# A Winograd convolution with batch norm and SiLU on one core: unit outputs in a tile of three parts, and a new order of work around the second unit

## The chip, the cores and the metric

The kernel runs on one core of one Trainium2 chip. The metric is the device time of one execution in microseconds, taken as the median of several; lower is better. A profile of one execution shows, for each engine, when each instruction ran.

The engines are TensorE (PE; its weight loads are shown apart as PEld), VectorE (DVE), ScalarE (ACT), GpSimd (POOL) and SyncE (SP, which here only issues DMAs).

## The reference

A convolution of width 3 along the sequence, then a batch norm with fixed statistics, then SiLU. x is 2 x 2048 x 1024, w is 3 x 1024 x 1024, both bfloat16.

```python
xp = jnp.pad(x, ((0, 0), (P, P), (0, 0)))
y = sum(jnp.einsum('bsc,cd->bsd', xp[:, k:k + S, :], w[k]) for k in range(K))
inv_std = 1.0 / jnp.sqrt(var + 1e-5)
y = (y - mean) * (g * inv_std) + b
return _silu(y)
```

## The kernel before

It is a Winograd scheme: six outputs along the sequence are made from eight products. 342 blocks of six cover a sequence of 2048.

**Stage 1, transforms.** For each of the two sequences, 17 windows of x come in by DMA, and TensorE multiplies them with the constant matrix Rm (line 230) into PSUM. ScalarE and VectorE copy the result to T_sb (lines 244 and 246): eight transformed values (j = 0 to 7) for each channel tile and block. In the second sequence a window is made in three thirds, and matmuls of unit 0 are put between them (lines 401 to 408, the generator `first`, advanced by `run(first, n)`).

**The weights.** The output channels come in eight chunks of 128 (dc = 0 to 7). For j = 0 and 7 the raw weights are used (tile wch). For j = 1 to 6 they are made by GpSimd: `pair_sum` adds the outer two taps (line 163), and `pair_tap` adds or subtracts the middle one (line 173) into the tile uch. That is three sums and six taps for a chunk. `scale_weights` makes scaled taps w2x, w1x, w0x on ScalarE (line 151). For chunks 2 to 7 the first of the three sums is made on VectorE by a reduction (`outer_by_reduce`, line 169). uch has two buffers, so the chunk that is made follows the chunk that is used.

**Stage 2, units.** A unit is one chunk of one sequence: 16 units, numbered 0 to 15, with chunk and sequence in that order (unit 2 is chunk 1 of the first sequence). A unit is eight groups of eight matmuls of 342 columns (line 255), in the order j = 1, 3, 2, 4, 5, 7, 6, 0. They go to four PSUM banks, called A, B, C and G: A1, B3, A2, B4, C5, G7, C6, A0. The even units use banks 0 to 3, the odd ones 4 to 7. Unit 0 has another order (its groups of 7 and 0 come in parts of 231 and 111 columns, its last group is C6), and the last unit is cut in two.

Between the groups, `copy_out` (line 303) lets ScalarE copy a bank to a tile: m1 after A1, m3 after B3, s1 after A2, s2 after B4, m5 after C5. A2 adds to bank A, which m1 must have been copied out of, and in the same way B4 follows m3, and C6 follows m5. VectorE then makes the six outputs y[0] to y[5] of the unit by sums with a factor (line 296): d1 after s1, then y[2] and y[4] after B4, then y[1], y[3], y[5], then y[5] with G (line 342), then y[2] and y[4] again after C6, y[1], y[3], y[5] again, and y[0] last, after A0.

**The order on ScalarE.** The finished outputs go through SiLU on ScalarE (`silu`, line 266) into yT, in three calls: outputs 2 and 4, then 1, 3 and 5, then 0. A unit does not issue its own calls, since its sums are not done. It leaves them in the list `late`, and the next unit takes them from there: `pace` says how many entries are taken ahead of each of its copies m1, m3, s1, s2, m5, and what is left is taken behind m5. With the usual pace (1, 0, 1, 1, 0) the order on ScalarE is call, m1, m3, call, s1, call, s2, m5. Unit 1 has (0, 1, 1, 1, 0). Behind the three calls stands `finish`, which issues the DMA transpose of yT on the SP queue (line 425) and the stores of the unit before (lines 439 and 443). There are two yT tiles, used in turns.

**The dependencies.** Each unit opens a new tile y with one buffer (line 292). Its first write waits until the calls on the tile before are all done. In that tile output i stands in row i, so the calls read rows with a step of two.

**Chunk 1.** While unit 1 runs, the weights of chunk 1 are made (line 476 to 478): `sums(0, 2, 1)` scales taps 2 and 1 and makes the first sum and two taps, `sums(1)` the second, and `sums(2, 0)` scales tap 0 (w0x) and makes the third; the last of these is put at the end of `late`. The weights of chunk 2 are made from unit 3 on in program order (lines 459 to 467), with its reduction on VectorE ahead of unit 2 (line 458).

Of the kernel before, what the change touches and what calls it, by code (L numbers as in the profile page):

```python
# [10 lines left out]
FP32 = mybir.dt.float32  # L11
# [17 lines left out]
BETA = -4.0 / 5.0  # L29
M_OUT = 6  # L30

ENDS = (2, 4, 0, 5, 1, 3)
NJ = 8
WT = 21
# [3 lines left out]
def kernel(  # L38
# [13 lines left out]
    P = 128  # L52
    CT = C // P
    DC = D // P
    assert S % P == 0 and C % P == 0 and D % P == 0
    NTB = (S + M_OUT - 1) // M_OUT
# [27 lines left out]
    def load_weights(dp):  # L84
        open_weights(dp)
        for k in (0, 2, 1):
            nc.sync.dma_start(out=pair_tile[dp][:, k], in_=w_all[:, k, :, dp * 2 * P:(dp + 1) * 2 * P])
# [174 lines left out]
            )  # L262
            yield

    def silu(dc, yT, y_all, c0, c1, i0, i1, step=1):
        nc.scalar.activation(  # L266
            yT[:, i0:i1:step, c0:c1],
            y_all[:, i0:i1:step],
            ACT.Silu,
            bias=beta[:, dc:dc + 1],  # L270
            scale=sk[:, dc:dc + 1],
        )

    def unit(dc, bi, c0, c1, banks, yT, late, pace=(1, 0, 1, 1, 0), cut=None, calls=None):

        nn = c1 - c0
        A, B_, C_, G = [ps_all[:, k * 512:k * 512 + nn] for k in banks]
        bA, bB, bC, bG = banks
        pace = list(pace)

        def et(name):
            return epool.tile([P, NTB], FP32, name=name)[:, 0:nn]

        m1, m3, m5, s1, s2, d1 = (et(n) for n in ("m1", "m3", "m5", "s1", "s2", "d1"))
        y_all = epool.tile([P, M_OUT, NTB], FP32, name="y")[:, :, 0:nn]
        y = [y_all[:, i if calls is None else ENDS.index(i)] for i in range(M_OUT)]

        def stt(o, i0, s, i1, op1=ALU.add):
            nc.vector.scalar_tensor_tensor(out=o, in0=i0, scalar=s, in1=i1, op0=ALU.mult, op1=op1)  # L296
            load["dve"] += 0.00123 * nn

        def copy_out(dst, src):
            for _ in range(pace.pop(0)):  # L300
                if late:
                    late.pop(0)()
            nc.scalar.copy(dst, src)  # L303
            load["act"] += 0.001 * nn

        if cut:


            p0 = et("s2")
            yield from mms(bG, 7, dc, bi, c0, c0 + cut, True)  # L310
            yield from mms(bC, 0, dc, bi, c0, c0 + cut, True)
            yield from mms(bC, 0, dc, bi, c0 + cut, c1, True, cut)
            copy_out(p0, C_)
        yield from mms(bA, 1, dc, bi, c0, c1, True)
        copy_out(m1, A)
        yield from mms(bB, 3, dc, bi, c0, c1, True)
        copy_out(m3, B_)
        yield from mms(bA, 2, dc, bi, c0, c1, False)
        copy_out(s1, A)
        stt(d1, m1, 2.0, A, op1=ALU.subtract)  # L320
        yield from mms(bB, 4, dc, bi, c0, c1, False)
        if cut:
            stt(y[0], B_, ALPHA, p0)
            stt(y[2], B_, ALPHA * 4.0, s1)
            nc.vector.tensor_tensor(y[0], A, y[0], op=ALU.add)
            stt(y[4], B_, ALPHA * 16.0, s1)
        else:
            copy_out(s2, B_)
            for i in (2, 4):
                stt(y[i], B_, ALPHA * 2.0 ** i, s1)  # L330
        stt(B_, m3, 2.0, B_, op1=ALU.subtract)
        yield from mms(bC, 5, dc, bi, c0, c1, True)
        copy_out(m5, C_)
        while late:
            late.pop(0)()
        for i in (1, 3, 5):
            stt(y[i], B_, ALPHA * 2.0 ** i, d1)
        if cut:
            yield from mms(bG, 7, dc, bi, c0 + cut, c1, True, cut)
        else:  # L340
            yield from mms(bG, 7, dc, bi, c0, c1, True)
        nc.vector.tensor_tensor(y[5], G, y[5], op=ALU.add)  # L342
        yield from mms(bC, 6, dc, bi, c0, c1, False)
        for i in (2, 4):
            stt(y[i], C_, BETA * 0.5 ** i, y[i])
        stt(G, m5, 2.0, C_, op1=ALU.subtract)
        if not cut:
            yield from mms(bA, 0, dc, bi, c0, c1, False)
        for i in (1, 3, 5):
            stt(y[i], G, BETA * 0.5 ** i, y[i])  # L350
        if cut:
            stt(y[0], C_, BETA, y[0])
        else:
            stt(y[0], s2, ALPHA, A)
            stt(y[0], C_, BETA, y[0])

        if calls is None:
            late.extend(lambda i=i: silu(dc, yT, y_all, c0, c1, *i, 2) for i in ((2, 5), (1, 6), (0, 1)))
        else:
            late.extend(lambda i=i: silu(dc, yT, y_all, c0, c1, *i) for i in calls)  # L360

    def run(gen, n=None):
        while n is None or n > 0:
            if next(gen, run) is run:
                return
            if n is not None:
                n -= 1
# [3 lines left out]
    with tc.tile_pool(name="xwin", bufs=10) as xpool:  # L371
        first = unit(0, 0, 0, NTB, (0, 1, 2, 3), yTs[0], late, cut=11 * WT)
        for wi in range(NWIN):
            window = load_window(xpool, 0, wi)
            if wi in (3, 8, NWIN - 1):
                load_chunk(0, {3: 2, 8: 0, NWIN - 1: 1}[wi])
            for h in range(2):
                bk = (2 * wi + h) % 4 * 2 if wi < 10 else (0, 6, 4)[(2 * wi + h - 20) % 3]
                transform(0, wi, window, 4 * h, 4, bk, 2, 2 if h == 0 and wi in (4, 9) else 0)
            if wi == 0:  # L380
                turn_params()
            if wi == 5:
                open_chunk(0)
                scale_weights(0, (2,), on_gpsimd=True)
            if wi == 8:
                pair_sum(0, 0)
                pair_sum(0, 1)
                scale_weights(0, (0,), on_gpsimd=True)
                pair_sum(0, 2)

            run(first, {13: 2, 14: 2, 15: 4, 16: 8}.get(wi, 0))
        pair_tap(0, 0, ALU.add)
        scale_weights(0, (1,), on_gpsimd=True)
        for n, op in ((1, ALU.add), (0, ALU.subtract), (1, ALU.subtract), (2, ALU.add), (2, ALU.subtract)):
            pair_tap(0, n, op)
        make_params()
        load["act"] = load["dve"] = 0.0
        gi, done = 0, 0


        for wi in range(NWIN):
            window = load_window(xpool, 1, wi)
            for ct0, n in ((0, 3), (3, 3), (6, 2)):
                transform(1, wi, window, ct0, n, 4 + gi if gi < 4 else (4, 5, 6, 7, 2)[(gi - 4) % 5], 3)
                gi += 1
                want = 8 * gi // 3 if gi < 4 else 8 + 20 * (gi - 3) // (3 * NWIN - 3)
                run(first, want - done)
                done = want
        for k in (0, 2, 1):
            load_chunk(1, k)  # L410
        load_weights(1)
        run(first)

    opool = ctx.enter_context(tc.tile_pool(name="opool", bufs=3))
# [36 lines left out]
            store_unit(*turned.pop(0))  # L451

    late.append(lambda: finish(0, 0, yTs[0]))
    for ui, (dc, bi) in enumerate(units[1:-1], 1):
        yT = yTs[ui % 2]
        half = 4 * (ui % 2)
        if bi == 0 and dc + 1 < DC:
            outer_by_reduce(dc + 1)
        if bi == 1 and dc + 1 < DC:
            open_chunk(dc + 1)  # L460
            if dc:
                scale_weights(dc + 1)
                for n in range(3):
                    if n:
                        pair_sum(dc + 1, n)
                    for op in (ALU.add, ALU.subtract):
                        pair_tap(dc + 1, n, op)
            else:

                def sums(n, *taps):  # L470
                    scale_weights(1, taps)
                    pair_sum(1, n)
                    for op in (ALU.add, ALU.subtract):
                        pair_tap(1, n, op)

                sums(0, 2, 1)
                sums(1)
                late.append(lambda: sums(2, 0))
        calls = ((0, 2), (2, 6)) if ui == len(units) - 2 else None
        run(unit(dc, bi, 0, NTB, (half, half + 1, half + 2, half + 3), yT, late, (1, 0, 1, 1, 0) if ui > 1 else (0, 1, 1, 1, 0), calls=calls))  # L480
        if ui < len(units) - 2:
            late.append(lambda dc=dc, bi=bi, yT=yT: finish(dc, bi, yT))
        if bi == 1 and dc % 2 == 1 and (dc + 3) // 2 < DC // 2:
            load_weights((dc + 3) // 2)
# [98 lines left out]
        copy(o_before[0:n1 - n0, :, nb], pv[0:n1 - n0])  # L583
    store_unit(*units[-2], lambda nb: o_before[:, :, nb])

    y2 = epool.tile([P, M_OUT, NTB], FP32, name="y")[:, :, 0:NTB - cut]
    second = last_part(cut, NTB, there, y2, {
        "s1": [lambda: silu(dc, yT, y1, 0, cut, 0, 3)],
        "m5": [lambda: silu(dc, yT, y1, 0, cut, 3, 6)],
# [46 lines left out]
```

## Time and profile before

| | us |
|---|---|
| median of three runs | 191.4 (191.17 to 191.7) |
| the profiled execution | 191.42 |
| its span, from the first to the last instruction | 189.7 |
| first matmul of unit 2 | 49.88 |
| first matmul of unit 3 | 59.60 |

The span is what the profile covers; some 1.7 us of the time lie outside of it. In the page's rows, a time behind the bar is busy time and mean duration, and what follows the second bar is the idle time ahead of the group with what ended it. In a timeline the columns are start, time from the first start to the last end, engine, line, operation, tiles written and read, shapes and count; rows of like instructions are merged. Matmuls are pipelined, so the distance of two starts is what one costs TensorE, and not its duration.

### The profile page before, as it was taken

The page shows a single profiled execution, that of the slowest core. Times are in us where ns is not written, and L with a number is a line of the kernel's source. Part 1 is how long each engine was busy: PE and PEld are TensorE (multiplying, and loading weights), DVE is VectorE, ACT ScalarE, POOL GpSimd, SP SyncE. Part 2 cuts the span into 40 slices and gives each one's busy share as a digit, 9 for nine tenths or more (in the row PEclk, how much of TensorE's full clock was granted, in tenths as well). Part 3 has the DMA queues.
Part 4 walks back from the last instruction along what each step waited for, and adds up shares of the span by engine and source line. Part 5 has one row for each costly group of instructions (what it writes and reads, how often), then busy time and mean ns, then how long its engine had stood idle before and what let it go on. Part 6 is the DMA issues. An engine that isn't in the chain of part 4 may idle for free.

```text
span 189.7 us, 3974 instructions
## 1 busy us (share of the span) xinstructions
PE 179.5 (95%) x1424; PEld 126.5 (67%) x1424; DVE 159.2 (84%) x342; ACT 123.0 (65%) x205; POOL 148.8 (78%) x91
## 2 busy tenths in 40 slices
PE   7887999999999999999999999999999999999960
PEld 3656889766666666666666666666666666669960
DVE  6567699796999799969996999699969987879980
ACT  3787799658387827862876387648755874534680
POOL 6529999999769997999699969996999699901010
PEclk9999999999999999999999999999999999999996
DMA  5999999950609197979292889793747465656345
GB/s 131 326 351 309 334 385 262 247 132 0 124 19 202 34 209 209 208 175 208 58 200 46 191 229 205 167 204 75 164 80 157 91 147 98 137 110 154 87 114 111
DMA packets 86757, 31.72 MB, mean 167 GB/s; under 512 B 73357, under 2 KB 82578, under 8 KB 86738
## 3 DMA queue, kind: packets, MB, share of 16 engines
q1 hardware_dynamic: 86637, 31.46, 70.6%
q8 instruction: 11, 0.18, 0.4%
q14 instruction: 9, 0.07, 0.1%
q10 hardware_dynamic: 68, 0.01, 0.0%
q0 software_dynamic: 32, 0.01, 0.0%
HBM read 14.82 MB, written 8.39 MB: 122 GB/s over the span
## 4 chain that ended last, share of the span: by engine, by line
PE 74%; DVE 10%; DMA 5%; ACT 4%; issue 3%; SPq 2%; DVEq 0%; ACTq 0%
PE ps_all L255 66%; PE ps_all L230 7%; DVE y L296 6%; DMA xw<-in_x_dram 5%; SPq L215 1%; ACT T_sb L244 1%; DVE ps_all L296 1%; ACT yT L266 1%; PE ps_all L499 1%; DVE y L342 1%; DVE T_sb L246 0%; ACT s L303 0%; SPq L90 0%; ACT o_end L594 0%; DVE e L169 0%
## 5 line engine op out<-in xcount | busy, mean ns | idle before, releaser
L255 PE MATMUL ps_all<-T_sb,uch 128*128 128x342 bf16 (+2 forms) x816 | 120.8, 299 | 0.7 <-ACT m L303 0.3
L255 PEld LDWEIGHTS <-uch 128*128 128x128 bf16 x816 | 77.0, 97 | 35.3 <-issue 1.5
L266 ACT ACTIVATE yT<-y,beta,sk 128x684 bf16<-128x684 f32 (+4 forms) x46 | 44.0, 959 | 27.0 <-DVE y L296 27.0
L255 PE MATMUL ps_all<-T_sb,wch 128*128 128x342 bf16 (+4 forms) x288 | 43.7, 292 | 0.0
L296 DVE SCALAR_TENSOR_TENSOR y<-ps_all,y 128x342 f32<-128x342 f32 x90 | 41.8, 507 | 1.0
L173 POOL TENSOR_TENSOR uch<-e,wch 128x1024 bf16<-128x1024 f32 x16 | 33.9, 2134 | 9.1 <-PE ps_all L255 4.7
L173 POOL TENSOR_TENSOR uch<-e,w1x 128x1024 bf16<-128x1024 f32 x16 | 33.8, 2130 | 0.6
L173 POOL TENSOR_TENSOR uch<-eh,w1x 128x1024 bf16<-128x1024 f32 x16 | 33.8, 2132 | 0.5
L255 PEld LDWEIGHTS <-wch 128*128 128x128 bf16 x288 | 26.7, 97 | 10.9
L303 ACT COPY m<-ps_all 128x342 f32<-128x342 f32 x45 | 19.8, 442 | 19.5 <-PE ps_all L255 19.0
L244 ACT CAST T_sb<-ps_all 128x672 bf16<-128x672 f32 (+5 forms) x48 | 26.0, 619 | 5.5 <-PE ps_all L230 5.1
L230 PE MATMUL ps_all<-Rm,xw 128*128 128x168 bf16 (+1 forms) x272 | 26.4, 236 | 2.1 <-DMA xw<-in_x_dram 0.9
L246 DVE CAST T_sb<-ps_all 128x504 bf16<-128x504 f32 (+4 forms) x37 | 24.0, 694 | 5.1 <-PE ps_all L230 4.2
L230 PEld LDWEIGHTS <-xw 128*128 128x128 bf16 (+1 forms) x272 | 20.7, 99 | 7.3 <-issue 2.5
L296 DVE SCALAR_TENSOR_TENSOR y<-ps_all,d 128x342 f32<-128x342 f32 x45 | 20.3, 508 | 0.5
L163 POOL TENSOR_TENSOR eh<-w0x,wch 128x1024 f32<-128x1024 bf16 x8 | 17.0, 2128 | 1.1 <-ACT w0x L151 1.0
L296 DVE SCALAR_TENSOR_TENSOR y<-ps_all,s 128x342 f32<-128x342 f32 x31 | 14.5, 508 | 3.4 <-ACT s L303 3.2
L163 POOL TENSOR_TENSOR e<-wch,w2x 128x1024 f32<-128x1024 bf16 x8 | 17.0, 2129 | 0.0
L296 DVE SCALAR_TENSOR_TENSOR d<-m,ps_all 128x342 f32<-128x342 f32 x15 | 7.6, 508 | 10.2 <-ACT s L303 10.2
L296 DVE SCALAR_TENSOR_TENSOR ps_all<-m,ps_all 128x342 f32<-128x342 f32 x30 | 15.3, 508 | 0.0
L169 DVE TENSOR_REDUCE e<-wch 128x1024 f32<-128x2048 bf16 x6 | 13.7, 2277 | 0.0
L303 ACT COPY s<-ps_all 128x342 f32<-128x342 f32 x30 | 13.1, 435 | 0.5 <-PE ps_all L255 0.5
(69 smaller groups left out, 85.9 us busy)
## 6 DMA issues: line engine op xcount, KB each, us to landing
xw<-in_x_dram SPq DMA_DIRECT2D x30, 256.0 KB
out_dram<-o_sb SPq DMA_DIRECT2D x30, 192.0 KB
wch<-in_w_dram SPq DMA_DIRECT2D x9, 512.0 KB
out_dram<-o_sb SPq DMA_DIRECT2D x15, 120.0 KB
wch<-in_w_dram SPq DMA_DIRECT2D x6, 256.0 KB
xw<-in_x_dram SPq DMA_DIRECT2D x2, 224.0 KB
out_dram<-o_sb SPq DMA_DIRECT2D x15, 7.5 KB
out_dram<-o_sb SPq DMA_DIRECT2D x15, 0.5 KB
```

Source lines behind the costliest of these rows:

```text
L163: engine.tensor_tensor(e, a, c, op=ALU.add)
L169: nc.vector.tensor_reduce(e, taps.rearrange("p k ct d -> p ct d k"), axis=mybir.AxisListType.X, op=ALU.add)
L173: nc.gpsimd.tensor_tensor(wts[dc][:, 2 * n + (op == ALU.subtract)], outer[dc, n], odd, op=op)
L215: nc.sync.dma_start(out=xw[0:kk, :], in_=x[bi, t_lo:t_hi + 1, :])
L230: nc.tensor.matmul(banks[:, at:at + NJ * ntile], lhsT=xw[0:kk, (ct0 + c) * P:(ct0 + c + 1) * P], rhs=Rm[0:kk, :, 0:ntile], start=True, sto ...
L244: nc.scalar.copy(dst, src)
L246: nc.vector.tensor_copy(dst, src)
L255: nc.tensor.matmul(ps_all[:, bk * 512 + at:bk * 512 + at + c1 - c0], lhsT=lhsT, rhs=T_sb[bi][:, ct, j, c0:c1], start=start and ct == 0, st ...
L266: nc.scalar.activation(yT[:, i0:i1:step, c0:c1], y_all[:, i0:i1:step], ACT.Silu, bias=beta[:, dc:dc + 1], scale=sk[:, dc:dc + 1],)
L296: nc.vector.scalar_tensor_tensor(out=o, in0=i0, scalar=s, in1=i1, op0=ALU.mult, op1=op1)
L303: nc.scalar.copy(dst, src)
L342: nc.vector.tensor_tensor(y[5], G, y[5], op=ALU.add)
```

## The change

1. All units share one tile y, made once. Its rows are ordered by the calls: outputs 2 and 4 first, then 0, then 1, 3 and 5 (`KEPT`). Each SiLU call reads adjacent rows, and a write needs only the calls on its own rows to be done. The last unit's second part uses the same tile.
2. Unit 1's pace is (0, 1, 0, 1, 1), and unit 2's is (0, 1, 1, 1, 0). `sums(2, 0)` stands at the head of `late`, so it is what unit 1 takes ahead of m3: w0x comes between m1 and m3, the first SiLU call ahead of s2, the second ahead of m5, the third behind it. In unit 2, m1 comes ahead of the first call.
3. Chunk 2's first sum is a `pair_sum` on GpSimd ahead of its taps; the reduction ahead of unit 2 is gone. Chunks 3 to 7 keep theirs.
4. Two matmuls of unit 0 come one third of a window sooner, in the last window of the second sequence. Ahead of unit 0's last group (C6) stand the first three matmuls of unit 1's A1 (`begun`, in bank 4).

```diff
+KEPT = (2, 4, 0, 1, 3, 5)
 ENDS = (2, 4, 0, 5, 1, 3)
...
-    def silu(dc, yT, y_all, c0, c1, i0, i1, step=1):
+    y_all = epool.tile([P, M_OUT, NTB], FP32, name="y")
+
+    def silu(dc, yT, y_from, c0, c1, i0, i1, outputs=None):
         nc.scalar.activation(
-            yT[:, i0:i1:step, c0:c1],
-            y_all[:, i0:i1:step],
+            yT[:, outputs or slice(i0, i1), c0:c1],
+            y_from[:, i0:i1, 0:c1 - c0],
...
-        y_all = epool.tile([P, M_OUT, NTB], FP32, name="y")[:, :, 0:nn]
-        y = [y_all[:, i if calls is None else ENDS.index(i)] for i in range(M_OUT)]
+        y = [y_all[:, (KEPT if calls is None else ENDS).index(i), 0:nn] for i in range(M_OUT)]
...
-        yield from mms(bA, 1, dc, bi, c0, c1, True)
+        yield from begun or mms(bA, 1, dc, bi, c0, c1, True)
...
-            late.extend(lambda i=i: silu(dc, yT, y_all, c0, c1, *i, 2) for i in ((2, 5), (1, 6), (0, 1)))
+            parts = ((0, 2, slice(2, 5, 2)), (3, 6, slice(1, 6, 2)), (2, 3, slice(0, 1)))
+            late.extend(lambda i=i: silu(dc, yT, y_all, c0, c1, *i) for i in parts)
...
-                want = 8 * gi // 3 if gi < 4 else 8 + 20 * (gi - 3) // (3 * NWIN - 3)
+                want = 8 * gi // 3 if gi < 4 else 8 + 20 * (gi - 3) // (3 * NWIN - 3) + 2 * (gi > 3 * NWIN - 3)
...
         load_weights(1)
+
+        run(first, 7 * CT - done)
+        begun = mms(4, 1, *units[1], 0, NTB, True)
+        run(begun, 3)
         run(first)
...
+    paces = {1: (0, 1, 0, 1, 1), 2: (0, 1, 1, 1, 0)}
...
-        if bi == 0 and dc + 1 < DC:
+        if bi == 0 and 2 < dc + 1 < DC:
             outer_by_reduce(dc + 1)
...
-                    if n:
+                    if n or dc == 1:
                         pair_sum(dc + 1, n)
...
-                late.append(lambda: sums(2, 0))
+                late.insert(0, lambda: sums(2, 0))
...
-        run(unit(dc, bi, 0, NTB, (half, half + 1, half + 2, half + 3), yT, late, (1, 0, 1, 1, 0) if ui > 1 else (0, 1, 1, 1, 0), calls=calls))
+        run(unit(dc, bi, 0, NTB, (half, half + 1, half + 2, half + 3), yT, late, paces.get(ui, (1, 0, 1, 1, 0)), None, calls, begun if ui == 1 else None))
...
-    y2 = epool.tile([P, M_OUT, NTB], FP32, name="y")[:, :, 0:NTB - cut]
+    y2 = y_all[:, :, 0:NTB - cut]
```

More of the change, by code (lines that the diff above doesn't have):

```diff
@@ L272, in silu, with unit @@
         )
-    def unit(dc, bi, c0, c1, banks, yT, late, pace=(1, 0, 1, 1, 0), cut=None, calls=None):
+    def unit(dc, bi, c0, c1, banks, yT, late, pace=(1, 0, 1, 1, 0), cut=None, calls=None, begun=None):
         nn = c1 - c0
```

## The prediction

> **What bounds the kernel now.** I read the page first, then the chain of waits in order of time, then TensorE's timeline around the places where that chain leaves TensorE.
>
> ```profile
> PE 179.5 (95%) x1424; PEld 126.5 (67%) x1424; DVE 159.2 (84%) x342; ACT 123.0 (65%) x205; POOL 148.8 (78%) x91
> PE 74%; DVE 10%; DMA 5%; ACT 4%; issue 3%; SPq 2%; DVEq 0%; ACTq 0%
> ```
>
> ```profile
> 62.15 115.58 PE ps_all L255 x816
> ```
>
> TensorE is busy for 95% of the span. The second fence is the chain in order of time: from 62.15 us it is TensorE alone for 115.58 us, so whatever makes that stretch begin sooner ends the kernel sooner, and nothing inside it can be gained by a change to other engines. What is left to gain lies ahead of 62.15. TensorE's timeline (start, time until the last one ends, count) shows it:
>
> ```profile
> 35.06 0.32 PE L255 MATMUL ps_all<-T_sb,uch 128*128 128x342 bf16 x1
> 35.31 0.30 PE L230 MATMUL ps_all<-Rm,xw 33*128 33x48 bf16 x5
> ...
> 38.61 0.55 PE L255 MATMUL ps_all<-T_sb,wch 128*128 128x111 bf16 x8
> 39.30 7.25 PE L255 MATMUL ps_all<-T_sb,uch 128*128 128x342 bf16 x48
> 46.40 1.32 PE L255 MATMUL ps_all<-T_sb,wch 128*128 128x342 bf16 x8
> ...
> 49.88 2.49 PE L255 MATMUL ps_all<-T_sb,uch 128*128 128x342 bf16 x16
> 52.64 3.64 PE L255 MATMUL ps_all<-T_sb,uch 128*128 128x342 bf16 x24 [0.28 <-ACT m L303]
> 56.12 1.32 PE L255 MATMUL ps_all<-T_sb,wch 128*128 128x342 bf16 x8
> ...
> 59.60 6.20 PE L255 MATMUL ps_all<-T_sb,uch 128*128 128x342 bf16 x40
> 65.64 1.32 PE L255 MATMUL ps_all<-T_sb,wch 128*128 128x342 bf16 x8
> ...
> 69.11 5.97 PE L255 MATMUL ps_all<-T_sb,uch 128*128 128x342 bf16 x40
> 74.93 1.32 PE L255 MATMUL ps_all<-T_sb,wch 128*128 128x342 bf16 x8
> ```
>
> ```profile
> L255 PE MATMUL ps_all<-T_sb,wch 128*128 128x111 bf16 x16 | 1.4, 213 | 0.0
> ```
>
> Matmuls overlap, so I go by starts. From 52.64 to 56.12 there are 24 of them: 3.48/24 = 0.145 us each, 1.16 us a group of eight, 9.28 a unit. With that step each row says when the next one should start: 35.06 + 0.145 = 35.21, it is 35.31 (0.10 lost); the eight narrow ones step by (0.55 − 0.21)/7 = 0.049, so 38.61 + 0.39 = 39.00, it is 39.30 (0.30 lost); 39.30 + 48 × 0.145 = 46.26, it is 46.40 (0.14); 49.88 + 16 × 0.145 = 52.20, it is 52.64 (0.44); 59.60 + 40 × 0.145 = 65.40, it is 65.64 (0.24). From 69.11, 74.91 is due and 74.93 comes: nothing. The five holes hold 1.22 us, all that this change can reach.
>
> Four of them have their cause on ScalarE, whose copy out of a bank must end before TensorE adds to that bank:
>
> ```profile
> 38.81 0.44 ACT L303 COPY m<-ps_all 128x342 f32<-128x342 f32 x1 [1.88 <-PE ps_all L255]
> ...
> 41.82 0.44 ACT L303 COPY m<-ps_all 128x342 f32<-128x342 f32 x1 [0.67 <-PE ps_all L255]
> 42.73 0.96 ACT L266 ACTIVATE yT<-y,beta,sk 128x684 bf16<-128x684 f32 x1 [0.47 <-DVE y L296]
> 43.60 0.42 ACT L303 COPY m<-ps_all 128x342 f32<-128x342 f32 x1
> 44.55 1.24 ACT L266 ACTIVATE yT<-y,beta,sk 128x1026 bf16<-128x1026 f32 x1 [0.53 <-DVE y L296]
> 45.70 0.42 ACT L303 COPY s<-ps_all 128x342 f32<-128x342 f32 x1
> 46.02 0.67 ACT L266 ACTIVATE yT<-y,beta,sk 128x342 bf16<-128x342 f32 x1
> ...
> 47.25 1.07 ACT L151 ACTIVATE w0x<-wch 128x1024 bf16<-128x1024 bf16 x1
> 51.30 0.96 ACT L266 ACTIVATE yT<-y,beta,sk 128x684 bf16<-128x684 f32 x1 [2.98 <-DVE y L296]
> 52.17 0.77 ACT L303 COPY m<-ps_all 128x342 f32<-128x342 f32 x2
> ...
> 60.81 0.96 ACT L266 ACTIVATE yT<-y,beta,sk 128x684 bf16<-128x684 f32 x1 [1.14 <-DVE y L296]
> 61.68 0.95 ACT L303 COPY m<-ps_all 128x342 f32<-128x342 f32 x2
> ```
>
> The copy at 38.81 (m5 of unit 0) ends at 39.25, just ahead of 39.30. The other three copies (m3 at 43.60, m1 at 52.17 and at 61.68) stand behind a SiLU call that waits for VectorE's last sums of the unit before. So VectorE is late, ScalarE waits in its queue for it, and TensorE for ScalarE.
>
> **The change part by part.** I place the changed program's queues on these rows. A copy starts 0.20 us behind its group (38.61 to 38.81), I allow up to 0.26.
>
> *Two matmuls sooner, three of unit 1 ahead of the last group.* No matmul is added. Two of unit 0's stand after the last window's first third, where 0.10 was lost: −0.10. Three of unit 1's first group stand behind the narrow ones: they start at 38.90, the last group of unit 0 follows at 38.90 + 0.435 = 39.335, and m5 ends at 39.15, so it isn't held. Before, it began at 39.30 with these three still to do: −0.40 for both holes. The three write bank 4, whose last transform is among those at 35.31, 3.6 us earlier.
>
> *Copies ahead of SiLU in unit 1, w0x sooner.* The last group of unit 0 ends at 40.495, the other five of A1 at 41.22; TensorE's groups then start at 41.22 (B3), 42.38 (A2), 43.54 (B4), 44.70 (C5), 45.86 (G7), 47.02 (C6), and unit 2 at 49.34. ScalarE: m1 at 41.45; w0x at its end, 41.9, by its 1.07 until 42.9; m3 42.9 to 43.3, 0.2 ahead of B4: the 0.14 are gone. s1 at 43.8, the two-part SiLU 0.32 later (45.70 to 46.02) at 44.1, s2 0.87 later (42.73 to 43.60) at 45.0, the three-part SiLU at 45.3, m5 1.15 later (44.55 to 45.70) at 46.45, done at 46.9. C6 needs it at 47.02. That is the tightest place of the change, 0.1 us; taken at nothing. If the calls took their whole durations (0.96, 0.43, 1.24) m5 would end at 47.2 and 0.2 be given back; ends −0.14 and +0.1 for this part, and I take −0.14, since the starts of like pairs are nearest.
>
> *Outputs in one tile of three parts.* It removes waits: the first sums of a unit need only the call on their own part, no longer the unit's last call.
>
> ```profile
> 43.16 1.78 DVE L296 SCALAR_TENSOR_TENSOR y<-ps_all,y 128x342 f32<-128x342 f32 x4
> ...
> 47.06 0.94 DVE L296 SCALAR_TENSOR_TENSOR y<-ps_all,s 128x342 f32<-128x342 f32 x2 [0.39 <-ACT s L303]
> ...
> 53.96 2.28 DVE L169 TENSOR_REDUCE e<-wch 128x1024 f32<-128x2048 bf16 x1
> ...
> 59.85 0.92 DVE L296 SCALAR_TENSOR_TENSOR y<-ps_all,y 128x342 f32<-128x342 f32 x2
> ```
>
> In unit 1 the sums of 47.06 can start when s1, B4 and the two-part call are done, 45.1; from there VectorE runs 1.9 us ahead of before, and stops only for TensorE. In unit 2, m1 comes ahead of any SiLU: A1 ends at 50.50, m1 at about 51.2, A2 is due at 51.66: −0.44.
>
> *Chunk 2's first sum on GpSimd.* Without the 2.28 us at 53.96, unit 2's sums on C6 start when that group ends, 49.34 + 7 × 1.16 = 57.46, near 57.7 instead of 59.85 (1.2 behind their group), and end at 58.6. ScalarE gets through m5 (55.4) and three scalings at 1.07 by 59.0. The SiLU ahead of unit 3's m1 then ends by 59.95, A1 ends at 59.78, so m1 runs 60.0 to 60.4 and A2 is due at 60.94: −0.24.
>
> ```profile
> 34.61 2.12 POOL L163 TENSOR_TENSOR e<-wch 128x1024 f32<-128x1024 bf16 x1
> ...
> 48.40 2.13 POOL L163 TENSOR_TENSOR eh<-w0x,wch 128x1024 f32<-128x1024 bf16 x1 [0.98 <-ACT w0x L151]
> ...
> 56.38 4.24 POOL L173 TENSOR_TENSOR uch<-e,wch 128x1024 bf16<-128x1024 f32 x2 [1.53 <-PE ps_all L255]
> ...
> 69.16 4.23 POOL L173 TENSOR_TENSOR uch<-eh,w1x 128x1024 bf16<-128x1024 f32 x2
> ```
>
> GpSimd pays 2.12 more (its like at 34.61), but w0x at 42.9 spares it the 0.98 ahead of 48.40, and 1.53 were idle ahead of 56.38 (the sum on VectorE ended at 56.24). So its taps of chunk 2 start at 56.38 − 0.98 − 1.53 + 2.12 + 0.1 (one more start) = 56.1, 0.3 sooner. The last it must meet is unit 4's C5, due at 69.11 + 4.64 − 1.22 = 72.53, whose tap (the first half of 69.16, done at 71.3) is now done at 71.0: 1.5 to spare. Were w0x no help, it would be 72.0, still in time. Cost nothing; beyond 1.5 late it would cost TensorE its whole lateness.
>
> A rule speaks against this step. The Trainium skill (SBUF — State Buffer, "SBUF: two separate sides") has GpSimd and VectorE lock a shared port pair for a whole instruction when VectorE reads two SBUF inputs. By it nothing happens to sums with one input in PSUM; were they locked all the same, the rival "GpSimd holds VectorE" below has the result.
>
> *The store of unit 0.*
>
> ```profile
> 46.76 11.30 SPq L425 DMA_TRANSPOSE o_sb<-yT  x2
> ```
>
> Its transpose starts when the one-part call ends, at 47.5 instead of 46.76; the call that writes that yT again comes at 58.6. SP has nothing else queued but the next transpose: no cost.
>
> Sum: 0.40 + 0.14 + 0.44 + 0.24 = 1.22. The profiled execution took 191.42 (span 189.7 and 1.7 around it); the median is 191.40. Forecast 191.42 − 1.22 = **190.2**.
>
> **The rivals.**
> *ScalarE's queue of unit 1 is the new wait.* For it: 0.1 us to spare at m5, and two SiLU calls, 2.2 us, now between s1 and m5. Against: both find their sums ready (44.94 was VectorE's last). If m5 is 0.3 to 0.5 late, 0.2 to 0.4 come back: 190.4 to 190.6.
> *GpSimd holds VectorE.* If its sum at 53.9 to 56.0 blocks VectorE, unit 2's sums are as late as under the reduction, and the 0.24 stay: 190.45. Against: the two sums at 59.85 took 0.92 us inside GpSimd's row from 56.38 to 60.62, the two at 47.06 took 0.94 while GpSimd was partly idle.
> *The start is sooner, the end isn't.* TensorE runs 1.22 ahead, GpSimd only 0.3; if a later chunk is late, or stores, most is given back: 190.9 to 191.4. Against: GpSimd needs 8 × 2.13 = 17.0 us for a chunk, TensorE 18.56, and it idles between chunks.
> *Slower: the SiLU calls on parts take longer.* They recur in all units; the place is m1 behind the two-part call:
>
> ```profile
> 69.45 0.96 ACT L266 ACTIVATE yT<-y,beta,sk 128x684 bf16<-128x684 f32 x1 [3.12 <-DVE y L296]
> ...
> 70.53 0.45 ACT L303 COPY m<-ps_all 128x342 f32<-128x342 f32 x1
> ```
>
> ```profile
> L266 ACT ACTIVATE yT<-y_end,beta,sk 128x687 bf16<-128x687 f32 x2 | 1.9, 966 | 0.0
> ```
>
> m1 ends at 70.98, A2 is due at 69.11 + 2.32 = 71.43: 0.45 to spare, the point from which it decides. Twice the 0.96 would cost 0.5 in some 11 units, 5.5 in all: 195.7. Against: a call that reads adjacent rows takes 966 ns for 687 elements, the strided one 0.96 us for 684.
>
> **How the numbers follow.** Forecast 68%, ScalarE's queue 15%, GpSimd holding VectorE 4%, end not sooner 9%, slower 4%. About 0.3% (0.57 us) can be told from no change here, so faster ends at 190.83. The first three lie below it; I take 7 points off for the spread of the runs (191.17 to 191.7) and larger sizes: faster 0.80, same 0.15, slower 0.05. The range: the forecast with that spread starts at 189.8; up to 190.9 any 0.7 us of the holes may stay open.
>
> **What would show it.** Right: no hole on TensorE between 35 and 66 us; unit 2's first matmul at 49.3 and unit 4's at 67.9; w0x near 41.9; GpSimd's new sum ahead of 56; VectorE without a reduction near 54. Wrong: a start of C6 in unit 1 behind 47.1 with m5 as releaser, a wait for uch in unit 4, or an end that did not move with 67.9.

## The result, and the profile after

The changed kernel takes 190.06 us (median of six runs, 189.64 to 190.36) beside 191.45 for the kernel before (six runs, 191.17 to 192.32): a ratio of 0.9919 with a 95% interval from 0.9896 to 0.9943. The forecast was 190.2. The profiled execution took 190.36, 1.06 less than the 191.42 of the one before; its span is 188.6 us.

The page's first row and its chain, and the one piece of the chain in order of time that answers to the 115.58 us of before. The changed file's lines are some further down: L257 is the line of the matmuls (L255 before), L309 the copies, L272 SiLU, L302 the sums.

```profile
PE 179.3 (95%) x1424; PEld 126.7 (67%) x1424; DVE 157.1 (83%) x341; ACT 122.8 (65%) x205; POOL 150.9 (80%) x92
PE 87%; DMA 5%; ACT 2%; SPq 2%; DVE 1%; issue 0%; ACTq 0%; DVEq 0%
```

```profile
35.92 140.74 PE ps_all L257 x995
```

The stretch in which nothing but TensorE sets the end now begins at 35.92 instead of 62.15. VectorE had 10% of the chain and has 1%. Its busy time is 2.1 us less and GpSimd's 2.1 more: the sum that moved. TensorE's timeline:

```profile
34.65 0.49 PE L232 MATMUL ps_all<-Rm,xw 128*128 128x168 bf16 x5
35.08 0.61 PE L257 MATMUL ps_all<-T_sb,uch 128*128 128x342 bf16 x3
35.62 0.30 PE L232 MATMUL ps_all<-Rm,xw 33*128 33x48 bf16 x5
...
38.62 0.56 PE L257 MATMUL ps_all<-T_sb,wch 128*128 128x111 bf16 x8
39.02 7.14 PE L257 MATMUL ps_all<-T_sb,uch 128*128 128x342 bf16 x48
45.99 1.32 PE L257 MATMUL ps_all<-T_sb,wch 128*128 128x342 bf16 x8
...
49.47 5.97 PE L257 MATMUL ps_all<-T_sb,uch 128*128 128x342 bf16 x40
58.76 5.97 PE L257 MATMUL ps_all<-T_sb,uch 128*128 128x342 bf16 x40
...
68.05 5.97 PE L257 MATMUL ps_all<-T_sb,uch 128*128 128x342 bf16 x40
```

Read with the same step of 0.145: 38.62 + 0.39 = 39.01, it is 39.02; 39.02 + 48 × 0.145 = 45.98, it is 45.99; unit 2 takes 58.76 − 49.47 = 9.29 and unit 3 takes 68.05 − 58.76 = 9.29, a unit without a hole (9.28). Four holes are gone. The first is not: 35.08 + 3 × 0.145 = 35.515, and the next matmul comes at 35.62.

The runs differ by about a microsecond in the part before, in which the windows come in by DMA: the narrow matmuls (the eight of 111 columns) start between 38.2 and 39.4 us in the thirteen profiles of this study. So I compare the stretch from the narrow matmuls to unit 4's first matmul, which holds the same matmuls in each kernel, except that three of them moved inside it. Before it is 69.11 − 38.61 = 30.50, after 68.05 − 38.62 = 29.43. The difference, 1.07, is the whole difference of the two executions (1.06).

ScalarE, VectorE and GpSimd in units 1 to 3:

```profile
41.88 1.06 ACT L153 ACTIVATE w0x<-wch 128x1024 bf16<-128x1024 bf16 x1
...
43.92 0.45 ACT L309 COPY s<-ps_all 128x342 f32<-128x342 f32 x1 [0.64 <-PE ps_all L257]
44.26 0.96 ACT L272 ACTIVATE yT<-y,beta,sk 128x684 bf16<-128x684 f32 x1
45.12 0.43 ACT L309 COPY s<-ps_all 128x342 f32<-128x342 f32 x1
...
46.59 0.44 ACT L309 COPY m<-ps_all 128x342 f32<-128x342 f32 x1
...
50.83 0.44 ACT L309 COPY m<-ps_all 128x342 f32<-128x342 f32 x1 [3.24 <-PE ps_all L257]
```

```profile
45.58 0.93 DVE L302 SCALAR_TENSOR_TENSOR y<-ps_all,s 128x342 f32<-128x342 f32 x2 [0.22 <-ACT s L309]
...
48.94 0.92 DVE L302 SCALAR_TENSOR_TENSOR y<-ps_all,y 128x342 f32<-128x342 f32 x2
...
58.19 0.93 DVE L302 SCALAR_TENSOR_TENSOR y<-ps_all,y 128x342 f32<-128x342 f32 x2
```

```profile
56.11 4.22 POOL L175 TENSOR_TENSOR uch<-e,wch 128x1024 bf16<-128x1024 f32 x2
...
68.88 4.22 POOL L175 TENSOR_TENSOR uch<-eh,w1x 128x1024 bf16<-128x1024 f32 x2
```

No SiLU call on ScalarE waits for VectorE in unit 1 any more, and m1 of unit 2 (50.83) waits for TensorE alone. The copies s1 and s2 of unit 1, which VectorE needs, come at 43.92 and 45.12 instead of 45.70 and 46.59. VectorE's sums on C6 come at 48.94 in unit 1 instead of 50.34, and at 58.19 in unit 2 instead of 59.85. GpSimd's taps of chunk 2 start at 56.11; 56.1 was worked out.

### The profile page after: what moved, and what is told of

Its sections match the earlier page's. It is cut to its first block, busy times and chain, and to the rows that moved or that the text cites. A ratio compares the mean times of both kernels' runs of the same rounds, so it can differ in the third digit from the quotient of the medians.

```text
span 188.6 us, 3960 instructions
## 1 busy us (share of the span) xinstructions
PE 179.3 (95%) x1424; PEld 126.7 (67%) x1424; DVE 157.1 (83%) x341; ACT 122.8 (65%) x205; POOL 150.9 (80%) x92
## 4 chain that ended last, share of the span: by engine, by line
PE 87%; DMA 5%; ACT 2%; SPq 2%; DVE 1%; issue 0%; ACTq 0%; DVEq 0%
PE ps_all L257 79%; PE ps_all L232 7%; DMA xw<-in_x_dram 5%; SPq L217 1%; ACT T_sb L246 1%; PE ps_all L513 1%; ACT yT L272 1%; DVE T_sb L248 0%; SPq L92 0%; ACT o_end L608 0%; DVE o_end L618 0%; ACT m L566 0%; ACTq L566 0%; DVEq L248 0%
## 5 line engine op out<-in xcount | busy, mean ns | idle before, releaser
L257 PE MATMUL ps_all<-T_sb,uch 128*128 128x342 bf16 (+2 forms) x816 | 120.3, 299 | 0.2 <-ACT m L566 0.2
L257 PEld LDWEIGHTS <-uch 128*128 128x128 bf16 x816 | 76.9, 97 | 34.2 <-issue 0.3
L272 ACT ACTIVATE yT<-y,beta,sk 128x684 bf16<-128x684 f32 (+4 forms) x46 | 44.0, 959 | 22.1 <-DVE y L302 22.1
L257 PE MATMUL ps_all<-T_sb,wch 128*128 128x342 bf16 (+4 forms) x288 | 43.7, 292 | 0.0
L302 DVE SCALAR_TENSOR_TENSOR y<-ps_all,y 128x342 f32<-128x342 f32 x90 | 41.8, 507 | 1.0
L309 ACT COPY m<-ps_all 128x342 f32<-128x342 f32 x45 | 19.9, 443 | 23.0 <-PE ps_all L257 22.5
L257 PEld LDWEIGHTS <-wch 128*128 128x128 bf16 x288 | 26.7, 97 | 10.9
L302 DVE SCALAR_TENSOR_TENSOR y<-ps_all,d 128x342 f32<-128x342 f32 x45 | 20.3, 508 | 0.6
L302 DVE SCALAR_TENSOR_TENSOR y<-ps_all,s 128x342 f32<-128x342 f32 x31 | 14.5, 508 | 3.5 <-ACT s L309 3.3
L302 DVE SCALAR_TENSOR_TENSOR d<-m,ps_all 128x342 f32<-128x342 f32 x15 | 7.6, 507 | 10.7 <-ACT s L309 10.7
L302 DVE SCALAR_TENSOR_TENSOR ps_all<-m,ps_all 128x342 f32<-128x342 f32 x30 | 15.3, 508 | 0.0
L309 ACT COPY s<-ps_all 128x342 f32<-128x342 f32 x30 | 13.1, 435 | 0.9 <-PE ps_all L257 0.9
L558 POOL TENSOR_TENSOR d<-m,s 128x229 f32<-128x229 f32 (+1 forms) x2 | 1.1, 554 | 14.0 <-ACT s L557 8.4
```

The lines of the kernel that those rows point to most:

```text
L257: nc.tensor.matmul(ps_all[:, bk * 512 + at:bk * 512 + at + c1 - c0], lhsT=lhsT, rhs=T_sb[bi][:, ct, j, c0:c1], start=start and ct == 0, st ...
L272: nc.scalar.activation(yT[:, outputs or slice(i0, i1), c0:c1], y_from[:, i0:i1, 0:c1 - c0], ACT.Silu, bias=beta[:, dc:dc + 1], scale=sk[:, ...
L558: nc.gpsimd.tensor_tensor(d1, m1, s1, op=ALU.subtract)
```

## The experiments

All of them are read by the stretch from the narrow matmuls to unit 4's first matmul: 30.50 us before, 29.43 in the changed kernel. Two profiles of the changed kernel give 29.43 and 29.42. The two versions with one unit's order changed, the one with an extra copy and the first one on the hole that stayed were executed once each, so only their traces are read.

### The early matmuls alone

The kernel before with the two edits to the program order of TensorE (`begun` is handed to unit 1 as in the change):

```diff
-                want = 8 * gi // 3 if gi < 4 else 8 + 20 * (gi - 3) // (3 * NWIN - 3)
+                want = 8 * gi // 3 if gi < 4 else 8 + 20 * (gi - 3) // (3 * NWIN - 3) + 2 * (gi > 3 * NWIN - 3)
...
+        run(first, 7 * CT - done)
+        begun = mms(4, 1, *units[1], 0, NTB, True)
+        run(begun, 3)
         run(first)
```

> The kernel before with part 4 of the change alone (two matmuls sooner, three of unit 1 ahead of unit 0's last group). Holes add up (the prediction's sum): the hole ahead of unit 0's last group closes, the others keep their size, and unit 4's first matmul comes at 68.7 to 68.8 instead of 69.11. Holes are in series behind VectorE: its queue of unit 0 runs without a stop and does not move, so m3 of unit 1 still ends at 44.0, the hole ahead of B4 grows from 0.14 to about 0.44, and unit 4 starts at 69.1 as before.

```profile
39.03 0.56 PE L255 MATMUL ps_all<-T_sb,wch 128*128 128x111 bf16 x8
39.43 4.81 PE L255 MATMUL ps_all<-T_sb,uch 128*128 128x342 bf16 x32
44.50 2.48 PE L255 MATMUL ps_all<-T_sb,uch 128*128 128x342 bf16 x16 [0.26 <-ACT m L303]
...
69.54 2.63 PE L255 MATMUL ps_all<-T_sb,uch 128*128 128x342 bf16 x17
```

TensorE's rows: the hole ahead of unit 0's last group is closed (39.03 + 0.39 = 39.42), and the one ahead of B4 has grown to 44.50 − 39.43 − 32 × 0.145 = 0.43. The stretch is 69.54 − 39.03 = 30.51, as before the change. The time is 191.49 us beside 191.43 (ratio 1.000, 0.998 to 1.002). What TensorE gains it waits for at the next copy. The chain of waits of the kernel before, in order of time, shows why:

```profile
37.64 0.93 DVE y L296 x2
...
43.16 1.37 DVE y L296 x3
...
45.70 0.42 ACT s L303
...
46.61 0.42 ACT s L303
...
47.06 0.94 DVE y L296 x2
...
61.68 0.43 ACT m L303
```

The chain leaves TensorE at 37.64, ahead of the four holes at the copies, and comes back to it at 62.15, at the end of the last of them. In between it runs on VectorE, except from 44.5 to 47.06, where ScalarE's three-part call, s1, one-part call and s2 stand in it, and at its end, where a SiLU call and m1 do. So the first three holes lie beside the chain, and filling the first alone moves nothing. The hole ahead of unit 0's last group isn't even VectorE's: its copy waited for TensorE's own group (1.88 us, at 38.81). The run with the early matmuls has the same chain; TensorE takes over at 62.58, 62.58 − 39.03 = 23.55 us behind the narrow matmuls, and before it is 62.15 − 38.61 = 23.54.

### The old order on ScalarE in units 1 and 2

```diff
-    paces = {1: (0, 1, 0, 1, 1), 2: (0, 1, 1, 1, 0)}
+    paces = {1: (0, 1, 1, 1, 0)}
...
-                late.insert(0, lambda: sums(2, 0))
+                late.append(lambda: sums(2, 0))
```

> The changed kernel with the order of before on ScalarE in units 1 and 2 (SiLU calls ahead of m3 in unit 1 and of m1 in unit 2, w0x last). Holes add up: 0.14 ahead of B4 in unit 1 and 0.44 ahead of A2 in unit 2 come back, unit 4 at 68.6. Holes in series: ahead of B4 in unit 1 stands 0.36, since m3 ends near 44.0 whatever TensorE does; ahead of A2 in unit 2 there is 0.1 or nothing, since VectorE starts unit 1's sums 0.5 sooner by the parts; unit 4 at 68.45.

```profile
39.27 0.56 PE L257 MATMUL ps_all<-T_sb,wch 128*128 128x111 bf16 x8
39.66 4.81 PE L257 MATMUL ps_all<-T_sb,uch 128*128 128x342 bf16 x32
44.73 2.48 PE L257 MATMUL ps_all<-T_sb,uch 128*128 128x342 bf16 x16 [0.26 <-ACT m L309]
...
50.53 2.49 PE L257 MATMUL ps_all<-T_sb,uch 128*128 128x342 bf16 x16
53.30 3.64 PE L257 MATMUL ps_all<-T_sb,uch 128*128 128x342 bf16 x24 [0.27 <-ACT m L309]
```

The hole ahead of B4 is 0.43, as for holes in series (0.36 was expected); but the one ahead of A2 in unit 2 is 53.30 − 50.53 − 2.32 = 0.45, in full, where 0.1 or nothing was expected. The stretch is 69.55 − 39.27 = 30.28, 0.22 less than before the change: only the 0.24 ahead of unit 3's A2 is gained, by the sum on GpSimd. The time is 191.17 us (ratio 0.998, 0.996 to 1.000). The expectation failed on VectorE, where the unit's first sums were to start half a microsecond sooner by the parts. VectorE's and ScalarE's rows of this run show why not:

```profile
47.72 0.93 DVE L302 SCALAR_TENSOR_TENSOR y<-ps_all,s 128x342 f32<-128x342 f32 x2 [0.39 <-ACT s L309]
```

```profile
46.68 0.67 ACT L272 ACTIVATE yT<-y,beta,sk 128x342 bf16<-128x342 f32 x1
47.26 0.43 ACT L309 COPY s<-ps_all 128x342 f32<-128x342 f32 x1
```

The sums start when the copy s2 ends, 47.69, and not when the SiLU call ends. The trace names a copy s as what released them, before the change and after it, and s2 is the one that ends just then. The sums read s1 and bank B, not s2; that they wait because the copy reads bank B too is not shown apart. So with unit 1's old order, in which the last call stands ahead of s2, the tile of parts frees nothing: the sums come 47.72 − 39.27 = 8.45 us behind the narrow matmuls, and before it is 47.06 − 38.61 = 8.45.

### A new tile for each unit, with the new order

```diff
-    y_all = epool.tile([P, M_OUT, NTB], FP32, name="y")
...
+        y_all = epool.tile([P, M_OUT, NTB], FP32, name="y")
         y = [y_all[:, (KEPT if calls is None else ENDS).index(i), 0:nn] for i in range(M_OUT)]
...
-    y2 = y_all[:, :, 0:NTB - cut]
+    y2 = epool.tile([P, M_OUT, NTB], FP32, name="y")[:, :, 0:NTB - cut]
```

> The changed kernel with a new tile y for each unit again (its rows still in the order of the calls), so that a unit's first sum waits for all calls of the unit before. One theory: the one-part call of unit 0, now behind m5, ends at 47.6, unit 1's sums start 2.0 us later than in the changed kernel, and two holes open, about 0.3 ahead of B4 in unit 2 and 0.2 ahead of A2 in unit 3: unit 4 at 68.5. Rival: these sums have 2 us to spare and nothing opens: 68.05.

```profile
48.37 0.93 DVE L302 SCALAR_TENSOR_TENSOR y<-ps_all,s 128x342 f32<-128x342 f32 x2 [2.26 <-ACT yT L271]
```

```profile
50.21 6.23 PE L257 MATMUL ps_all<-T_sb,uch 128*128 128x342 bf16 x40
...
59.75 2.49 PE L257 MATMUL ps_all<-T_sb,uch 128*128 128x342 bf16 x16
62.52 3.65 PE L257 MATMUL ps_all<-T_sb,uch 128*128 128x342 bf16 x24 [0.28 <-ACT m L309]
```

Unit 1's first sums now wait 2.26 us for the one-part call, which the new order puts behind m5. Two holes open, 6.23 − 5.97 = 0.26 in unit 2 and 62.52 − 59.75 − 2.32 = 0.45 ahead of A2 in unit 3; the first has the size that was expected, the second is twice as large. The stretch is 69.49 − 39.36 = 30.13, the time 191.15 us (ratio 0.998, 0.996 to 1.000). All of the change but the parts is worth 0.37 of the 1.07, and all of it but the new orders, in the run before, 0.22. Together they make 1.07.

### Unit 1's old order with unit 2's new pace, and the other way round

```diff
-    paces = {1: (0, 1, 0, 1, 1), 2: (0, 1, 1, 1, 0)}
+    paces = {1: (0, 1, 1, 1, 0), 2: (0, 1, 1, 1, 0)}
...
-                late.insert(0, lambda: sums(2, 0))
+                late.append(lambda: sums(2, 0))
```

> The changed kernel with unit 1's old order (SiLU call ahead of m3, w0x last) and unit 2's new pace (m1 ahead of the calls). From the narrow matmuls to unit 4's first matmul: 30.28 in the run with both old, 29.43 in the changed kernel. If m1's place in unit 2 alone closes the 0.44: the hole ahead of B4 in unit 1 is 0.42 still, none ahead of A2 in unit 2, 29.85. If VectorE's lateness only moves to the next copy: a hole of 0.2 or more ahead of B4 in unit 2, behind m3, 30.1 or more.

The stretch is 68.03 − 38.20 = 29.83, with one hole:

```profile
38.59 4.81 PE L257 MATMUL ps_all<-T_sb,uch 128*128 128x342 bf16 x32
43.65 2.49 PE L257 MATMUL ps_all<-T_sb,uch 128*128 128x342 bf16 x16 [0.26 <-ACT m L309]
```

43.65 − 38.59 − 4.64 = 0.42. VectorE is as late here as before the change: its sums on C6 of unit 1 come 49.92 − 38.20 = 11.72 us behind the narrow matmuls (50.34 − 38.61 = 11.73). So m1 ahead of the call in unit 2 does close the 0.44 by itself, as the prediction had it. In the other run only unit 2 has its usual pace:

```diff
-    paces = {1: (0, 1, 0, 1, 1), 2: (0, 1, 1, 1, 0)}
+    paces = {1: (0, 1, 0, 1, 1)}
```

> The changed kernel with the usual pace in unit 2, so that a SiLU call stands ahead of m1 there as before; unit 1 keeps its new order. The prediction put the 0.44 ahead of A2 in unit 2 down to m1 coming first: then a part of it is back. The other theory: VectorE is 1.9 us ahead by unit 1's order, that call's sums end near 49.9, the call near 50.8, when A1 ends too: no hole, and from the row of eight narrow matmuls to unit 4's first matmul it is 29.4 us as in the changed kernel (30.5 in the one before).

No hole, 68.11 − 38.70 = 29.41. ScalarE's rows there:

```profile
49.97 0.96 ACT L272 ACTIVATE yT<-y,beta,sk 128x684 bf16<-128x684 f32 x1 [2.31 <-DVE y L302]
50.96 0.45 ACT L309 COPY m<-ps_all 128x342 f32<-128x342 f32 x1
```

The call still waits for VectorE, but is done when A1 is. The edit in unit 2 is a second cover for a hole that unit 1's order closes too.

### Chunk 2's first sum back on VectorE

```diff
-        if bi == 0 and 2 < dc + 1 < DC:
+        if bi == 0 and dc + 1 < DC:
...
-                    if n or dc == 1:
+                    if n:
```

> The changed kernel with chunk 2's first sum back on VectorE. The prediction: without the move the 0.24 ahead of unit 3's A2 stay, unit 4 at 68.3 instead of 68.05. The other theory: VectorE is 1.9 us ahead in unit 1 by the new order, a reduction of 2.28 from 52.6 to 54.9 puts d1 of unit 2 off by 0.9 and its sums on C6 by 0.5 only, the SiLU ahead of m1 ends near 60.5, m1 near 60.9, and A2 is due at 61.1: no hole, unit 4 at 68.05, and GpSimd's taps of chunk 2 a microsecond sooner than 56.11.

```profile
58.38 0.92 DVE L302 SCALAR_TENSOR_TENSOR y<-ps_all,y 128x342 f32<-128x342 f32 x2
```

No hole: the stretch is 67.97 − 38.55 = 29.42. The reduction starts at 52.49, and unit 2's sums on C6 come 58.38 − 38.55 = 19.83 us behind the narrow matmuls, 0.26 later than in the changed kernel (58.19 − 38.62 = 19.57). GpSimd's taps of chunk 2 start at 54.90, 1.2 us sooner. The time is 190.46 us (ratio 0.9933, 0.9909 to 0.9957). The move of the sum closes the 0.24 where VectorE is late (the old order above), and nothing where it is not.

Then both of these edits were left out together, so that the early matmuls, the tile of parts and unit 1's order remain:

> The changed kernel with chunk 2's first sum back on VectorE and unit 2's usual pace: of the change, the early matmuls, the tile of three parts and unit 1's order are left. Each of the two alone opened no hole. If unit 1's order gives VectorE enough lead for both: no hole, 29.4 us from the narrow matmuls to unit 4, and the time of the changed kernel, 190.1 to 190.4. If the two cover for each other: a hole ahead of A2 in unit 2 or 3 of 0.2 or more.

The stretch is 68.07 − 38.65 = 29.42, the time 190.25 us (ratio 0.9941, 0.9919 to 0.9963). Half of the change makes all of the gain. No run leaves the early matmuls out of this half, so what they add to it is not shown.

### The margin at m5 of unit 1

```diff
+        if begun:
+            nc.scalar.copy(et("spare"), m1)
         copy_out(m5, C_)
```

> The changed kernel with one more ScalarE copy of 128x342 (m1 to a spare tile, used by nothing) ahead of m5 in unit 1. There m5 ends at 47.03 and C6 starts at 47.15 in the changed kernel. If the margin is 0.1, as predicted: m5 comes 0.33 later, a hole of 0.2 to 0.25 stands ahead of C6 in unit 1, and narrow matmuls to unit 4 take 29.65 to 29.7. If ScalarE has more to spare than the rows show, no hole and 29.43.

```profile
46.07 1.32 PE L257 MATMUL ps_all<-T_sb,wch 128*128 128x342 bf16 x8
47.53 1.32 PE L257 MATMUL ps_all<-T_sb,uch 128*128 128x342 bf16 x8
```

```profile
47.04 0.44 ACT L309 COPY m<-ps_all 128x342 f32<-128x342 f32 x1
```

The hole ahead of C6 is 47.53 − 46.07 − 1.16 = 0.30, and the stretch 68.42 − 38.70 = 29.72, 0.29 longer. m5 (the second fence, ScalarE) starts at 47.04 instead of 46.59; TensorE's rows stand 46.07 − 45.99 = 0.08 later in this run, so the copy cost ScalarE 0.37 (0.33 was expected), and the margin was 0.37 − 0.30 = 0.07. It is there, and hardly anything fits into it: the rest of what is put on ScalarE ahead of that copy is paid by TensorE.

### The hole that stayed

First the last window's thirds in one piece, with the matmuls behind them:

```diff
-                want = 8 * gi // 3 if gi < 4 else 8 + 20 * (gi - 3) // (3 * NWIN - 3) + 2 * (gi > 3 * NWIN - 3)
+                want = 8 * gi // 3 if gi < 4 else 8 + 20 * (gi - 3) // (3 * NWIN - 3)
+                if 3 * NWIN - 3 < gi < 3 * NWIN:
+                    want = done
```

> The changed kernel with the last window's three thirds in one piece, the matmuls of unit 0 that stood between them behind the last third. The hole of 0.1 ahead of the second third is there before and after the change, whatever number of matmuls stands ahead of it. If it is the cost of going from matmuls of 128 rows to those of 33: it comes once instead of twice, and from the last group of full windows (34.65) to the narrow matmuls (38.62) it is 3.86 instead of 3.97 us. If the second third waits for its bank's copy: the hole stays or grows, 3.97 or more.

```profile
34.86 0.91 PE L232 MATMUL ps_all<-Rm,xw 128*128 128x168 bf16 x10
...
38.90 0.56 PE L257 MATMUL ps_all<-T_sb,wch 128*128 128x111 bf16 x8
```

From 34.86 to 38.90 it is 4.04 us, 0.07 more than the 3.97 (the eight matmuls of 33 rows are merged into the first row). By itself this speaks for a wait on the banks' copies, and these are late: the second and the third piece start at 35.34 and 35.55, each 0.05 behind the end of the copy out of its bank (35.29 and 35.50). It does not tell such a wait alone from a switch of rows plus a wait. So in the next run four matmuls stand ahead of the last window, to give the copies time, and the thirds stay in one piece. Against the changed kernel:

```diff
-                want = 8 * gi // 3 if gi < 4 else 8 + 20 * (gi - 3) // (3 * NWIN - 3) + 2 * (gi > 3 * NWIN - 3)
+                want = 8 * gi // 3 if gi < 4 else 8 + 20 * (gi - 3) // (3 * NWIN - 3)
+                if gi >= 3 * NWIN - 3:
+                    want = 30
```

> The changed kernel with four matmuls of unit 0 ahead of the last window and its three thirds in one piece behind them, so that the banks' copies have 0.58 us to end. If the step from 128 rows to 33 costs 0.1 each time and the two holes of the run before were copies not yet ended: one step alone, no other hole, and from the last matmuls of full windows to the narrow ones 3.87 us instead of 3.97. If the copies are late here too: 3.97 or more. The time: 0.1 us at most, less than the runs scatter.

```profile
34.44 0.31 PE L232 MATMUL ps_all<-Rm,xw 128*128 128x168 bf16 x2
34.59 0.74 PE L257 MATMUL ps_all<-T_sb,uch 128*128 128x342 bf16 x4
35.26 0.39 PE L232 MATMUL ps_all<-Rm,xw 33*128 33x48 bf16 x8
35.58 2.79 PE L257 MATMUL ps_all<-T_sb,uch 128*128 128x342 bf16 x18
38.21 0.56 PE L257 MATMUL ps_all<-T_sb,wch 128*128 128x111 bf16 x8
```

From 34.44 to 38.21 it is 3.77 us, 0.20 less than in the changed kernel and twice what was expected. 34.59 + 4 × 0.145 = 35.17, and the first matmul of 33 rows comes at 35.26: 0.09 lost. Eight of these, 0.19 each, step by (0.39 − 0.19)/7 = 0.03, so the last starts at 35.46, and the next of 128 rows at 35.58, again 0.09 more than a step. The changed kernel goes from 128 rows to 33 and back twice, this one once, and each way costs 0.09; with the rows the width changes too, to 48 columns. In the run before, the thirds in one piece saved 0.2 and lost some 0.27 to copies that had not ended.

This version takes 190.11 us (189.7 to 190.69, ratio 0.9928 with 0.9909 to 0.9947), and the changed kernel, run beside it, 190.58 (190.26 to 190.94, ratio 0.9952 with 0.9934 to 0.9971).

> The changed kernel itself, run beside the two others: 29.43 us from the narrow matmuls to unit 4, 190.1 us.

Its stretch is 68.61 − 39.19 = 29.42. The two intervals overlap, and the changed kernel's own medians in two sets of runs, 190.06 and 190.58, are further apart than the 0.20 that the trace shows. So the 0.20 are shown in the trace, and not in the time.

## Why the prediction was right, point by point

- *TensorE from 62.15 on is what sets the end, and the holes ahead of it are the reach.* Right: the 1.07 us gained between the narrow matmuls and unit 4 are the 1.06 of the whole execution.
- *0.10 by two matmuls sooner.* Wrong. The hole is not a wait that a matmul can fill; it is what TensorE takes to go from 128 rows to 33. This is the main term that separates the 1.22 of the sum from the 1.07 measured; the other 0.05 is no more than four holes read from rows of two decimals can be off (0.30, 0.14, 0.44 and 0.24 make 1.12).
- *0.30 by three matmuls of unit 1, 0.14 by unit 1's order, 0.44 by unit 2's pace, 0.24 by the sum on GpSimd.* The sum of the four holds; that each edit brings its own share does not. Added one after another, the early matmuls bring nothing, then the sum on GpSimd (with the parts) 0.23, unit 2's pace 0.45 and unit 1's order 0.40 (30.51, 30.28, 29.83, 29.43). Yet the early matmuls, the parts and unit 1's order bring all of it without the other two. The holes are places where TensorE stands beside one longer chain, through VectorE and ScalarE, and it is the last of them that sets the end. So an edit brings its own hole when the holes behind it are already closed: with the sum moved, TensorE takes over the chain at unit 2's A2 (53.30 in that run), with unit 2's pace too at unit 1's B4 (43.65). Or one edit shortens the chain itself: unit 1's order, which needs the tile of parts, closes the three holes behind SiLU calls at once, and the early matmuls have closed the first. Either way TensorE runs without a stop from the narrow matmuls on, and that is why the sum holds. The rows that told it were in the chain of waits ahead of 62.15, and the prediction used only the piece behind.
- *Unit 1's sums from 45.1 on, VectorE 1.9 us ahead.* They start at 45.58, and VectorE is 1.4 ahead (48.94 instead of 50.34). What the prediction had wrong is that the first sums need only s1, B4 and the two-part call. They wait for s2 as well.
- *m5 with 0.1 to spare.* Right: 0.07. The rival of a new wait on ScalarE was that close.
- *GpSimd's taps at 56.1, C5's tap at 71.0, nothing paid.* Right: 56.11, and 68.88 + 4.22/2 = 70.99. GpSimd did not hold VectorE either: its new sum ran from 53.91 to 56.04, and VectorE's two sums at 54.90, inside it, took 0.94, as the two at 47.06 before, when GpSimd was partly idle. The SiLU calls on parts take 0.96 and 1.25, as before (0.96 and 1.24).
- *190.2 us.* That the number came within 0.14 of the median is partly luck: the changed kernel's second set of runs gave 190.58, and the sum counts a hole of 0.10 that stayed.

## What to carry to other kernels

Several short holes of the busiest engine may be places where it stands beside one longer chain on other engines; filling the first then only widens the next. The chain of waits tells: if it stays on the other engines from before the first hole to the last, the holes together are still what can be gained, but what one edit brings depends on the others. Look for the edit that shortens the chain, and test each of the others without it. Here a dependency made finer freed nothing under the old order of work, and without it the new order, with the rest of the change, brought only 0.37 of 1.07.

## What the runs showed of the hardware

- Going from matmuls of 128 rows to matmuls of 33 cost TensorE 0.09 us, and going back 0.09 again, in each of the profiles; matmuls put in between did not hide it. The width changes with the rows here (48 columns); going from 342 columns to 111 at 128 rows cost nothing (35.58 + 18 × 0.145 = 38.19, it is 38.21 in the rows of the version with four matmuls ahead). The Trainium skill (TensorEngine Tiling (Array Packing), "Key Properties") says that changing the tiling mode drains the engine. The rows agree, if 33 rows make another mode than 128; that the drain is what takes the 0.09 us was not tried apart.
- VectorE's first sums of a unit and ScalarE's copy s2 read the same bank, and the sums start when the copy has ended (45.12 + 0.43 = 45.55, sums at 45.58). The Trainium skill (PSUM — Partial Sum Buffer, "PSUM bank collisions raise a hardware error") counts two reads of one bank by two engines as a collision. No run here has them at once, so it can't be seen. In the changed kernel this wait is 0.22 us in unit 1 and 0.39 in eight units more; in units 4, 6, 8, 10 and 12, ahead of which VectorE makes a chunk's first sum, it is nothing.
